# Strassen products in the first batch's second feed-forward, a third buffer of probabilities, and early loads held back

## Chip, cores and metric

One core of a Trainium2 chip runs the whole program. The metric is the device time of one execution in microseconds (us): the median of three runs is given, and one further execution was recorded by the profiler.

## What is computed

Clustered attention, then a feed-forward block, then a mixture of four experts, all in fp32, two batches of 768 tokens (8 heads of 64, model width 512). The reference, cut:

```python
mask = q_assign[:, :, :, None] == k_assign[:, :, None, :]      # argmax over 16 centroids
scores = np.where(mask, scale * q @ k.T, -1e9)
attn = softmax(scores); x = (attn @ v)                          # (1536, 512)
h = x @ w_in                                                    # 512 -> 2048
x = (h * np.clip(h + 3, 0, 6) / 6) @ w_out
p = domain_probs / domain_probs.sum(-1)
for e in range(4):
    out += p[:, e:e+1] * (np.maximum(x @ w1[e], 0) @ w2[e])     # 512 -> 1024 -> 512
```

## The kernel before

Every fp32 product of the feed-forwards is made of three f16 matmuls (high by high, high by low, low by high), so each operand is first scaled and split into a high and a low f16 half. The work stands in five stretches: attention of batch 0 (`Attn(0)`, lines 551 to 755); the first feed-forward of batch 0 (`Moe1`, line 1067, four chunks of 512 hidden columns); the second one of batch 0 (`Moe2`, line 1160, eight chunks of 512, two to an expert), with the attention of batch 1 laid between its matmuls; then `Moe1` and `Moe2` of batch 1.

In a chunk the first layer multiplies 512 inputs by 512 hidden columns for two blocks of 384 tokens. The plain way (`g1`, with `mm3`, line 949) does 2 blocks x 4 column groups x 4 input groups x 3 matmuls of 128x384, 96 in all. The class `Wino` (line 962) does the same with seven products in place of eight, 84 matmuls: `sums_w` (line 906) builds four sums of weight quarters (DVE, line 912) and splits them into `ws` (ACT, line 915; DVE, line 916), `sums_x` (line 966) builds four sums of token quarters (line 976) and splits them into `tx`, and `g1w` (line 1013) runs the products in PSUM tiles `psw`, copying partial results out (ACT into `keep`, line 1042; DVE, lines 1044 and 1049). Before the change only chunks 1 and up of the second batch use it. Both token blocks must then have one scale: `Moe1.split` (line 1148) writes the split input `x2h`, `x2l` at each block's own scale, and for batch 1 once more, as `x2hw`, `x2lw`, at the common one. The second layer (`g2`, line 1200) is 6 tiles x 12 matmuls of 128x512 into `psm`, added to `oa` by DVE (line 1218).

Attention works in sets: four matmuls (`pss`, lines 808 and 810) into a tile of two PSUM banks, a row maximum (DVE, `ut`, line 815), the exponential with its row sum (ACT, `e`, line 816), the normalised halves. In batch 0 (`turned`) the normalised row is turned by TensorE (`pst`, line 728); the normalising itself (line 716) is on POOL or DVE as the letters of `kn` say. In batch 1 (`block`) the two f16 halves `p` (lines 831 to 839) are turned by a DMA (`pt<-p`). At the start `Attn.prep` loads `raw` (q and k of a head, line 577), ACT and DVE split it into `qa`, `qb`, `ka`, `kb`, and the cluster numbers reach `qb` and `kb` through `ohq` and `pso` (lines 646 to 660). `vmax` (line 677) loads V (`vr`) and takes its largest value. `conv_w` (line 923) loads the weights of the first feed-forward (`r`, 512 KB each) and converts them.

The order on every engine is fixed when the program is built: `Order.plan` (line 244) plays the tasks through with costs of its own and places, on each engine, the task that can start first, ties and near ties by a priority; `PAR` (line 39) holds the priorities' offsets, pool sizes and choices of engine. All loads go through one queue, SP's. The engines then run these orders strictly.

Of the kernel before, what the change touches and what calls it, by code (L numbers as in the profile page):

```python
# [9 lines left out]
F32 = mybir.dt.float32  # L10
# [13 lines left out]
XSC = 8.0  # L24
# [3 lines left out]
def _f32(u):  # L28
# [14 lines left out]
    wx=4.354846549739053,  # L43
    wxs=1.369895543634687,
    wl=4.57673773750327,
    slack=0.05,
    ahead=2.5,
    wait=0,
    wait0=0.0,
    until=20.0,  # L50
    wgap=4,
    ta=33.19699973099627,
    tu=2.5993853998990764,
    lead0=23.93963461472225,
    lead2=1.4339520625967201,
    vlead2=5.517029808375997,
    lead1=2.337584274393799,
    vlead=-42.625279365213466,
    avp=-5.763899395482756,
    parts=3,  # L60
    avpa=-7.810000648567701,
    kn='PDPPDP',
    kt='AAADA',
    kb='PAAD',
    gl=["DDDD", "DDDD"],
    mx=27.33314733110412,
    sp=9.847346224163463,
    spc=7.092455914465626,
    wse=dict(i="P", o="S", **{"1": "P", "2": "A"}),
    v0=15.554800497248644,  # L70
# [9 lines left out]
    r64p=5.115084205662186,  # L80
    slow=1.0713800859542972,
    psx=3,
    dup=["SSSS", "P"],
    dpx=2,
    trp=2.509280866509063,
    trh=2,
    parta=6,
    cv0=136.14562710937315,
    cvd=15.713217770054491,
    cva=2,  # L90
    cvb=(3, 8, 4),
    wo1=0,
    two=[0, 0],
    seq=[0, 1, 3, 2, 4, 5, 6, 7, 9, 10, 11, 8],
    btail=6.718647286749997,
    bu0=40.95307569041337,
    bdu=37.26759314364028,
    bvl=14.96118549196903,
    bpr=6.461926094972937,
# [42 lines left out]
class Order:  # L142
# [101 lines left out]
    def plan(self):  # L244
# [18 lines left out]
        while left:  # L263
# [106 lines left out]
def body(ctx: ExitStack, tc: tile.TileContext, qk, vd, cent, w_in, w_out, probs, w1, w2, out):  # L370
# [36 lines left out]
    def dma(nbytes, prio, fn, r, w, lag=0.0):  # L407
        return add("SP", 0.52, prio, fn, r, w, dma=nbytes / 360e3, lag=lag)
# [32 lines left out]
    p_s = [Pool("ps_sa", 2, g_pa, True), Pool("ps_sb", 2, g_ps, True)]  # L441
# [32 lines left out]
    xv = fixed([128, B, 4], F32, "xv")  # L474
    xsc = fixed([128, B, 4], F32, "xsc")
# [51 lines left out]
    def allmax(am, n, inv, ki, unit, sc, ks, p, pp):  # L527
# [8 lines left out]
        dve(1, p, lambda: nc.vector.tensor_scalar(out=inv, in0=inv, scalar1=1e-30, scalar2=unit, op0=ALU.max, op1=ALU.mult), [], [ki])  # L536
        dve(1, p, lambda: nc.vector.reciprocal(out=sc, in_=inv), [ki], [ks])
# [13 lines left out]
    class Attn:  # L551
# [299 lines left out]
    def split_w(key, raws, p, dst=None):  # L851
        _, _, sc, ks = wcol(*key[1:])
        for k, raw in enumerate(raws):
            w = Buf(dst or (p_wi if key[1] in "i1" else p_wo), [128, 2, 512], F16, "w")
            how = PAR["wse"][key[1]]
            if how in "SPA" and (how != "S" or key[1] in "i1" and key[2] and (key[1] == "i" or key[0])):
# [4 lines left out]
                act(512, p, lambda w=w, raw=raw: nc.scalar.activation(out=w[:, 0], in_=raw.t, func=AF.Copy), [raw], [(w, 0)])  # L861
                pool(512, p, lambda w=w, raw=raw: nc.gpsimd.tensor_tensor(out=w[:, 1], in0=raw.t, in1=w[:, 0], op=ALU.subtract), [raw, (w, 0)], [(w, 1)])  # L862
# [43 lines left out]
    def sums_w(key, raws, p):  # L906
        for k in range(2):
# [5 lines left out]
            for x in (u, v):  # L913
                w = Buf(p_ws, [128, 2, 512], F16, "ws")
# [8 lines left out]
    def conv_w(key, src, p, pp):  # L923
# [3 lines left out]
        for k in range(4):  # L927
# [4 lines left out]
                out=r.t, in_=src[:, k].bitcast(I32).rearrange("p (n t) -> p n t", t=2)), [], [r])  # L932
# [29 lines left out]
    class Wino:  # L962
        bank, line = p_w, ""


        def sums_x(self, p):

            t = self.tx = [[Buf(p_tx, [128, 2, MB], F16, f"tx{i}") for _ in range(2)] for i in range(4)]
# [44 lines left out]
        def g1w(self, c, i, ts):  # L1013
# [357 lines left out]
```

## Time and profile before

| | |
|---|---|
| time, median of 3 runs | 982.29 us (979.53 to 982.61) |
| the profiled execution | 981.2 us, of which the span from the first to the last instruction is 979.3 us |
| PE matmul, PE weight load | 931.9 us (95%), 553.4 us (57%) |
| DVE, ACT, POOL | 680.0 us (69%), 622.7 us (64%), 356.8 us (36%) |
| chain that ended last | PE 67%, DVE 11%, ACT 9%, DMA 7% |
| TensorE's granted clock | 1.00 throughout |

The busy time of an engine is the union of its instructions' durations. Matmuls overlap their neighbours, so a matmul's listed duration is not what one more of them costs. DVE is VectorE, ACT ScalarE, POOL GpSimd, SP the queue that issues the DMAs.

### The profile page before, as it was taken

What the parts mean: (1) busy time and instruction counts of PE and PEld (TensorE: products, weight loads), DVE (VectorE), ACT (ScalarE), POOL (GpSimd) and SP (SyncE); (2) the same over time, 40 slices, a digit from 0 to 9 for tenths busy, and PEclk for the clock granted to TensorE, in tenths of its full rate; (3) what the DMA queues carried; (4) which work ended last, traced back from release to release, by engine and by line L of the source; (5) the groups of instructions that cost most, each with busy time, mean ns of one, the idle gap of its engine ahead of it and who ended that gap; (6) DMA issues with size and microseconds to landing.
All of it is one profiled execution on the core that took longest, in us unless ns stands there. A gap on an engine that the chain in (4) does not pass through costs nothing.

```text
span 979.3 us, 16082 instructions
## 1 busy us (share of the span) xinstructions
PE 931.9 (95%) x5699; PEld 553.4 (57%) x5699; DVE 680.0 (69%) x1427; ACT 622.7 (64%) x1243; POOL 356.8 (36%) x380
## 2 busy tenths in 40 slices
PE   2889999999999999999999999999999999999998
PEld 1667775665655655655565565556655455555554
DVE  6988896888767774674586666956589766654643
ACT  4798987768677876595496455555467455556421
POOL 0554734334534554544365221000232354344200
PEclk9999999999999999999999999999999999999999
DMA  8343438786425773484285378432111122212001
GB/s 235 88 128 85 142 104 311 265 272 229 172 98 142 152 145 124 96 168 120 61 184 127 106 140 193 141 128 69 64 65 65 56 75 87 71 59 86 1 1 65
DMA packets 123952, 120.45 MB, mean 123 GB/s; under 512 B 81440, under 2 KB 81440, under 8 KB 123872
## 3 DMA queue, kind: packets, MB, share of 16 engines
q1 hardware_dynamic: 123872, 119.43, 42.8%
q8 instruction: 45, 0.74, 0.3%
q14 instruction: 35, 0.29, 0.1%
HBM read 79.75 MB, written 14.68 MB: 96 GB/s over the span
## 4 chain that ended last, share of the span: by engine, by line
PE 67%; DVE 11%; ACT 9%; DMA 7%; issue 3%; POOL 3%; ACTq 0%; POOLq 0%; DVEq 0%; SPq 0%
PE psm L954 9%; PE psm L956 9%; PE psm L955 9%; PE psg L954 6%; PE psg L955 6%; PE psg L956 6%; PE psw L1032 4%; DMA pt<-p 4%; PE psw L1034 4%; PE psw L1033 4%; ACT e L816 3%; PE psv L744 2%; PE pst L728 2%; DVE p L839 2%; PE pss L808 2%
## 5 line engine op out<-in xcount | busy, mean ns | idle before, releaser
L862 POOL TENSOR_TENSOR w<-wraw,w 128x512 f16<-128x512 f32 x128 | 146.7, 1164 | 162.5 <-ACT w L861 128.2
L954 PE MATMUL psm<-w,h 128*128 128x512 f16 x384 | 145.8, 380 | 3.7 <-DVE oa L1218 2.5
L956 PE MATMUL psm<-w,h 128*128 128x512 f16 x384 | 145.7, 379 | 1.5 <-DVE h L1196 1.4
L955 PE MATMUL psm<-w,h 128*128 128x512 f16 x384 | 145.6, 379 | 0.0
L816 ACT ACTIVATE e<-pss,ut 128x768 f32<-128x768 f32 x96 | 86.2, 899 | 36.6 <-DVE ut L815 31.2
L954 PEld LDWEIGHTS <-w 128*128 128x128 f16 x704 | 69.4, 99 | 50.2 <-issue 7.5
L861 ACT ACTIVATE w<-wraw 128x512 f16<-128x512 f32 x128 | 77.5, 625 | 30.2 <-POOL wraw L860 16.9
L954 PE MATMUL psm<-x2h,w 128*128 128x384 f16 x288 | 94.4, 328 | 2.2 <-DVE oa L1216 1.5
L955 PEld LDWEIGHTS <-w 128*128 128x128 f16 x704 | 68.9, 98 | 48.0 <-issue 6.2
L956 PEld LDWEIGHTS <-w 128*128 128x128 f16 x704 | 68.8, 98 | 47.4 <-issue 1.8
L1218 DVE SCALAR_TENSOR_TENSOR oa<-psm,pq,oa 128x512 f32<-128x512 f32 x84 | 62.4, 746 | 47.0 <-PE psm L956 46.6
L815 DVE TENSOR_REDUCE ut<-pss 128x1 f32<-128x768 f32 x96 | 90.9, 949 | 5.8 <-PE pss L810 5.2
L955 PE MATMUL psm<-x2l,w 128*128 128x384 f16 x288 | 93.9, 326 | 0.6 <-DVE x2l L1156 0.6
L956 PE MATMUL psm<-x2h,w 128*128 128x384 f16 x288 | 93.9, 326 | 0.0
L955 PE MATMUL psg<-g,w 128*128 128x384 f16 x256 | 83.5, 326 | 0.5 <-DVE g L1106 0.5
L954 PE MATMUL psg<-g,w 128*128 128x384 f16 x256 | 83.5, 326 | 0.3 <-ACT g L1105 0.3
L860 POOL TENSOR_SCALAR wraw<-wraw,wsc 128x512 f32<-128x512 f32 x64 | 45.2, 713 | 105.3 <-DMA wraw<-in_w 37.4
L956 PE MATMUL psg<-g,w 128*128 128x384 f16 x256 | 83.5, 326 | 0.0
L808 PE MATMUL pss<-ka,qa 128*128 128x384 f32 x192 | 61.8, 404 | 8.5 <-ACT e L816 5.2
L956 PEld LDWEIGHTS <-h 128*128 128x128 f16 x384 | 37.5, 98 | 48.7 <-DVE h L1196 4.0
L954 PEld LDWEIGHTS <-h 128*128 128x128 f16 x384 | 38.2, 99 | 44.5 <-issue 3.8
L1042 ACT ACTIVATE keep<-psw 128x384 f32<-128x384 f32 x60 | 29.2, 487 | 52.9 <-PE psw L1034 52.8
(192 smaller groups left out, 2157.1 us busy)
## 6 DMA issues: line engine op xcount, KB each, us to landing
wraw<-in_w SPq DMA_DIRECT2D x128, 256.0 KB, 3.2
r<-in_w_in SPq DMA_DIRECT2D x16, 512.0 KB, 5.0
r<-in_w_out SPq DMA_DIRECT2D x16, 512.0 KB, 4.3
w<-hl_i SPq DMA_DIRECT2D x32, 256.0 KB, 3.1
w<-hl_o SPq DMA_DIRECT2D x32, 256.0 KB, 4.3
raw<-in_qk SPq DMA_DIRECT2D x16, 384.0 KB, 3.7
hl_i<-w SPq DMA_DIRECT2D x16, 256.0 KB, 3.2
hl_o<-w SPq DMA_DIRECT2D x16, 256.0 KB, 2.2
```

What stands on the lines that cost most here:

```text
L808: nc.tensor.matmul(ps[:, f, 0:HS], qa[:, qs], ka[:, f * HS:f * HS + HS], start=True, stop=False)
L815: dve(S, p, lambda: nc.vector.tensor_reduce(out=nb(), in_=ps[:, :, 0:HS], axis=AX.XY, op=ALU.max, negate=True), [ps], [(tb, n)])
L816: act(S, p, lambda: nc.scalar.activation(out=e.t.rearrange("p (a b) -> p a b", a=2), in_=ps[:, :, 0:HS], func=AF.Exp, bias=nb(), scale=1.0 ...
L860: pool(512, p, lambda raw=raw: nc.gpsimd.tensor_scalar(out=raw.t, in0=raw.t, scalar1=sc, scalar2=1.0, op0=ALU.mult, op1=ALU.mult), [ks], [ ...
L861: act(512, p, lambda w=w, raw=raw: nc.scalar.activation(out=w[:, 0], in_=raw.t, func=AF.Copy), [raw], [(w, 0)])
L862: pool(512, p, lambda w=w, raw=raw: nc.gpsimd.tensor_tensor(out=w[:, 1], in0=raw.t, in1=w[:, 0], op=ALU.subtract), [raw, (w, 0)], [(w, 1)])
L954: nc.tensor.matmul(o_, ah, bh, start=i == 0, stop=False)
L955: nc.tensor.matmul(o_, ah, bl, start=False, stop=False)
L956: nc.tensor.matmul(o_, al, bh, start=False, stop=i == 3)
L1032: nc.tensor.matmul(o_, ah, bh, start=not more and k == 0, stop=False, skip_group_check=more)
L1033: nc.tensor.matmul(o_, ah, bl, start=False, stop=False, skip_group_check=more)
L1218: dve(512, p, lambda: nc.vector.scalar_tensor_tensor(out=oa[:, t], in0=ps.t, scalar=q, in1=oa[:, t], op0=ALU.mult, op1=ALU.add), [ps, qk], ...
```

## The change

The second feed-forward of batch 0 runs chunks 2 to 7 (`w0=2`) through `g1w`. For that `Moe1.g2` makes the second block's scale the common one (`least` in `allmax`), so that only block 0 is written a second time, and pools are added: `ws0` (4), `gw0` (4) and `ps_wc`, two PSUM banks, which are taken from the attention of batch 1: its score tiles go from two to one (`psb=1`). Product 2 of a chunk goes to `psm`'s banks. Of the weights of such a chunk the half that only the sums use is not split any more (`whole`). The attention of batch 1 has three `p` buffers in place of two, and reads V a second time instead of keeping it (`vr=2`). In the plan, a DMA's buffers count as free 0.91 or 1.22 us after its end in place of 0.15, DMAs run at 340 in place of 360 bytes a ns, two of the four first V loads may not start ahead of 12.3 us and the weights' loads not ahead of 16.0 us. `kn` puts all normalising of batch 0 on POOL, `dup` two more copies of `ka`. The other numbers of `PAR` are new offsets of the plan.

```diff
-    kn='PDPPDP',
+    kn='PPPPPP',
-    b_pool=dict(raw=2, vr=4, sc=2, ..., p=2, ...),
+    b_pool=dict(raw=2, vr=2, sc=1, ..., p=3, ...),
-    dup=["SSSS", "P"],
+    dup=["PSSS", "P"],
+    vre=2, nbv=12.297, nbr=16.026, psb=1, ws0=4, gw0=4, w0=2,
...
-                b.end = max(b.end, end + 0.15)
+                b.end = max(b.end, end + (0.15 if not t.dma else 1.22 if t.cols < 0 else 0.91))
-    def dma(nbytes, prio, fn, r, w, lag=0.0):
-        return add("SP", 0.52, prio, fn, r, w, dma=nbytes / 360e3, lag=lag)
+    def dma(nbytes, prio, fn, r, w, lag=0.0, start=0.0):
+        t = add("SP", 0.52, prio, fn, r, w, dma=nbytes / 340e3, lag=lag)
+        t.ready = start
+        return t
...
-    p_s = [Pool("ps_sa", 2, g_pa, True), Pool("ps_sb", 2, g_ps, True)]
+    p_s = [Pool("ps_sa", 2, g_pa, True), Pool("ps_sb", PAR["psb"], g_ps, True)]
-    p_w = Pool("ps_w", 5, g_pf, True)
+    p_w = [Pool("ps_wc", 4 - 2 * PAR["psb"], g_ps, True), Pool("ps_w", 5, g_pf, True)]
...
+        if least:
+            dve(1, p, lambda: nc.vector.tensor_tensor(out=inv, in0=inv, in1=least[0], op=ALU.max), [least[1]], [ki])
...
+            vr = self.buf("vr", [128, 2, NT, D], F32)
+            dma(393e3, max(p(0), self.seen + 0.1 * hp), lambda: nc.sync.dma_start(out=vr.t, in_=vd[b, hp]), [], [vr])
...
+            c = 512 if whole or k > 1 else 256
...
-        split_w(key, raws, p - PAR["sp"])
+        split_w(key, raws, p - PAR["sp"], None, not sums, sums)
+        if sums:
+            sums_w(key, raws, p)
...
-                    ps = Buf(self.bank, [128, 512], F32, "psw", self.line)
+                    ps = Buf(*((p_m, [128, 512], F32, "psw", "moe") if not self.b and j == 2 else (p_w[self.b], [128, 512], F32, "psw")))
...
-                    self.split(self.x2, blk, blk, p)
-                    if b and blk == NMB - 1:
...
-                        for k in range(NMB):
-                            self.split(x2w, k, 2, p + 8 + 4 * k)
+                    self.split(x2s[b][blk], blk, blk, p)
+                    if blk:
+                        self.split(x2w[b], 0, 1, p + G["xw"][b])
...
-                load_w(key, lambda k: src[:, k], p)
+                load_w(key, lambda k: src[:, k], p, n == "1" and self.wino(c))
-        wino = lambda self, c: self.b == 1 and c > 0
-        src = lambda self: [stages[2].acc]
-        xs = lambda self: x2w
+        wino = lambda self, c: c >= (1 if self.b else PAR["w0"])
+        src = lambda self: [stages[2].acc] if self.b else self.xs()[0]
```

What this moves is seen in the orders of the engines' instructions. First ACT near the start: `qa`, `ka` split a head's q and k, `qb<-pso` puts the cluster numbers into the first pair's keys, `wconv` takes up a weight. Before:

```order
L581 ACTIVATE qa<-raw 64x768
L619 ACTIVATE sc<-psc 128x384
L592 ACTIVATE ka<-raw 64x768
L934 ACTIVATE wconv<-r_274 128x512
L581 ACTIVATE qa<-raw 64x768
L658 ACTIVATE qb<-pso 16x768 x2
L592 ACTIVATE ka<-raw 64x768
```

And now:

```order
L597 ACTIVATE qa<-raw 64x768
L635 ACTIVATE sc<-psc 128x384
L608 ACTIVATE ka<-raw 64x768
L597 ACTIVATE qa<-raw 64x768
L608 ACTIVATE ka<-raw 64x768
L674 ACTIVATE qb<-pso 16x768 x2
L597 ACTIVATE qa<-raw 64x768
```

The weight (`wconv`) has gone from ahead of the first `qb` to behind the first exponential; the third head's `qa` still stands ahead of `qb`, and its `ka` now too. On SP's queue, which issues the loads, the rows behind the first two `raw` and the probabilities were:

```order
L683 DMA vr<-in_vd 128x768 x4
L931 DMA r_274<-in_w_in 128x1024
L582 DMA qb<-qa 64x768 x2
L595 DMA ka<-ka 64x768
L577 DMA raw<-in_qk 128x768
```

and are now:

```order
L700 DMA vr<-in_vd 128x768 x2
L598 DMA qb<-qa 64x768 x2
L593 DMA raw<-in_qk 128x768 x2
L700 DMA vr<-in_vd 128x768 x2
L598 DMA qb<-qa 64x768
```

Two V loads and a weight's load of 512 KB no longer stand ahead of the third `raw`. Third, DVE in the second feed-forward of batch 0, from one row maximum (`ut<-pss`) of batch 1's attention to the next. Before:

```order
L815 TENSOR_REDUCE ut<-pss 128x1
L839 SCALAR_TENSOR_TENSOR p<-e,ut,p 128x768
L824 TENSOR_SCALAR ut<-ut 128x1
L1196 SCALAR_TENSOR_TENSOR h<-psm_5019,h 128x384
L825 RECIPROCAL ut<-ut 128x1
L815 TENSOR_REDUCE ut<-pss 128x1
```

And now, in a chunk whose weight sums fall there:

```order
L834 TENSOR_REDUCE ut<-pss 128x1
L563 RECIPROCAL wsc<-wv 128x1
L934 TENSOR_TENSOR wraw<-wraw 128x256
L858 SCALAR_TENSOR_TENSOR p<-e,ut,p 128x768
L843 TENSOR_SCALAR ut<-ut 128x1
L934 TENSOR_TENSOR wraw<-wraw 128x256
L844 RECIPROCAL ut<-ut 128x1
L934 TENSOR_TENSOR wraw<-wraw 128x256 x2
L834 TENSOR_REDUCE ut<-pss 128x1
```

Four sums of weight quarters now lie between two maxima that had one `h` between them.

## Rows read from the trace of the kernel before

**Rows 1.** The page, busy time: engine, us (share of the span), instructions.
```profile
PE 931.9 (95%) x5699; PEld 553.4 (57%) x5699; DVE 680.0 (69%) x1427; ACT 622.7 (64%) x1243; POOL 356.8 (36%) x380
```
**Rows 2.** Stretches: length, busy us (x instructions) of PE, PEld, DVE, ACT, POOL; clock; DMA.
```profile
25.00:137.00 112.00, 103.37 (x729) 78.77 (x721) 99.44 (x235) 98.76 (x216) 61.10 (x63) 1.00 0.37 109
137.00:278.00 141.00, 137.34 (x870) 84.49 (x869) 110.40 (x229) 106.48 (x225) 55.44 (x68) 1.00 0.65 224
278.00:612.00 334.00, 325.31 (x2077) 191.51 (x2075) 221.66 (x453) 220.16 (x434) 142.63 (x146) 1.00 0.58 136
```
**Rows 3.** Timeline of PE, 479.7 to 484.9 us: start, duration, instruction.
```profile
479.85 0.33 PE L955 MATMUL psm<-x2l,w 128*128 128x384 f16 x1
...
481.31 0.33 PE L955 MATMUL psm<-x2l,w 128*128 128x384 f16 x1
```
**Rows 4.** Timeline of PE, ACT and DVE at the start: start, duration, instruction [idle before].
```profile
14.53 0.82 PE L653 MATMUL pso<-ident_b,ohq 128*128 128x128 bf16 x6 [5.48 <-DVE ohq L646]
...
21.87 1.01 PE L810 MATMUL pss<-kb,qb 80*128 80x384 f32 x2 [2.58 <-DVE kb L660]
...
8.83 0.33 SPq L577 DMA_DIRECT2D raw<-in_qk  x1
...
19.16 0.84 ACT L581 ACTIVATE qa<-raw 64x768 fp32r<-64x768 f32 x1 [3.13 <-DMA raw<-in_qk]
20.03 0.80 ACT L658 ACTIVATE qb<-pso 16x768 fp32r<-16x768 bf16 x1
```
**Rows 5.** The page, DMA issues: KB each, median us from issue to landing.
```profile
raw<-in_qk SPq DMA_DIRECT2D x16, 384.0 KB, 3.7
```
**Rows 6.** Groups of instructions: busy us, mean ns | idle before. Normalising in batch 0's attention.
```profile
L716 POOL TENSOR_SCALAR e<-e,ut 128x768 f32<-128x768 f32 x36 | 35.2, 984 | 42.9 <-ACT pt L735 12.8 <-DVE ut L824 10.4 <-DVE ut L825 8.0
L716 DVE TENSOR_SCALAR e<-e,ut 128x768 f32<-128x768 f32 x12 | 7.8, 649 | 0.1
```
**Rows 7.** Groups, whole run: the kinds of work that the change adds or cuts.
```profile
L862 POOL TENSOR_TENSOR w<-wraw,w 128x512 f16<-128x512 f32 x128 | 146.7, 1164 | 162.5 <-ACT w L861 128.2
L956 PE MATMUL psm<-x2h,w 128*128 128x384 f16 x288 | 93.9, 326 | 0.0
L912 DVE TENSOR_TENSOR wraw<-wraw 128x256 f32<-128x256 f32 x80 | 31.6, 424 | 1.4 <-POOL w L862 1.0
L1042 ACT ACTIVATE keep<-psw 128x384 f32<-128x384 f32 x60 | 29.2, 487 | 52.9 <-PE psw L1034 52.8
L916 DVE TENSOR_TENSOR ws<-wraw,ws 128x512 f16<-128x512 f32 x40 | 26.7, 691 | 0.2 <-ACT ws L915 0.2
L915 ACT ACTIVATE ws<-wraw 128x512 f16<-128x512 f32 x40 | 23.1, 621 | 21.8 <-DVE wraw L912 20.3 <-DVE p L839 1.3
L1049 DVE TENSOR_TENSOR psw<-psw,keep 128x384 f32<-128x384 f32 x40 | 22.4, 561 | 18.0 <-PE psw L1034 17.6 <-ACT keep L1042 0.3
L1156 DVE SCALAR_TENSOR_TENSOR x2l<-acc,xsc,x2h 128x384 f16<-128x384 f32 x16 | 8.8, 610 | 0.2 <-ACT x2h L1154 0.2
```
**Rows 8.** Line L976: ns min/median/max, first and last start.
```profile
L976 DVE TENSOR_TENSOR keep<-x1h,keep x4: 541/543/865, 619.5 to 633.9; 128x384 f32<-128x384 f16 x4
```
**Rows 9.** Timelines of PE, DVE and ACT, 487.6 to 490.8 us: one score set.
```profile
487.60 0.65 PE L808 MATMUL pss<-ka,qa 128*128 128x384 f32 x2
...
488.64 0.96 DVE L815 TENSOR_REDUCE ut<-pss 128x1 f32<-128x768 f32 x1
...
489.70 0.90 ACT L816 ACTIVATE e<-pss,ut 128x768 f32<-128x768 f32 x1 [0.82 <-DVE ut L825]
...
490.28 0.65 PE L808 MATMUL pss<-ka,qa 128*128 128x384 f32 x2
```
**Rows 10.** Waits of PE, 278 to 612 us: us in total, times, longest us.
```profile
PE psv L790 <- DMA pt<-p: 2.6, 3, 1.2
PE psm L954 <- DVE oa L1218: 2.5, 3, 1.2
```
**Rows 11.** Wait of ACT, 278 to 612 us.
```profile
ACT p L835 <- DMA pt<-p: 11.6, 10, 2.6
```

More of the change, by code (lines that the diff above doesn't have):

```diff
@@ L42 @@
     wsl="DD",
-    wx=4.354846549739053,
-    wxs=1.369895543634687,
-    wl=4.57673773750327,
+    wx=-1.1522284557866715,
+    wxs=1.4523186816394191,
+    wx0=43.37150067903462,
+    wl=7.46084025153843,
     slack=0.05,
+    vre=2,
+    nbv=12.297071615165793,
+    nbr=16.02553508875921,
+    xw=[4.0, 8.0],
     ahead=2.5,
     wait=0,
-    wait0=0.0,
+    wait0=0.8,
     until=20.0,
     wgap=4,
[L52 to L59, printed above, removed]
+    ta=33.594464710837215,
+    tu=2.610847985583524,
+    lead0=24.37119650954177,
+    lead2=1.612592269486031,
+    vlead2=-5.510083383690325,
+    lead1=2.0943943567986207,
+    vlead=-47.653832407507394,
+    avp=-10.148156292544726,
     parts=3,
-    avpa=-7.810000648567701,
-    kn='PDPPDP',
+    avpa=-4.563255851914643,
+    kn='PPPPPP',
     kt='AAADA',
-    kb='PAAD',
+    kb='AAPD',
     gl=["DDDD", "DDDD"],
-    mx=27.33314733110412,
-    sp=9.847346224163463,
-    spc=7.092455914465626,
+    mx=28.217289639625243,
+    sp=15.01076876764054,
+    spc=8.604011088911196,
     wse=dict(i="P", o="S", **{"1": "P", "2": "A"}),
-    v0=15.554800497248644,
+    v0=9.16094046643471,
     lr=0.3,
@@ L92 @@
     wo1=0,
-    two=[0, 0],
[L94 to L99, printed above, removed]
+    psb=1,
+    ws0=4,
+    gw0=4,
+    w0=2,
+    wr=8,
+    wob=8,
+    two=[0, 0],
+    seq=[0, 1, 3, 2, 5, 4, 6, 7, 9, 10, 11, 8],
+    btail=7.85293067823645,
+    bu0=40.446540415353034,
+    bdu=31.34254887856145,
+    bvl=4.7901688951714965,
+    bpr=6.264441884379736,
 )
@@ L682, in vmax @@
                 self.pair[hp]["vr"] = vr
-                dma(393e3, p(hp), lambda hp=hp, vr=vr: nc.sync.dma_start(out=vr.t, in_=vd[b, hp]), [], [vr])
+                dma(393e3, p(hp), lambda hp=hp, vr=vr: nc.sync.dma_start(out=vr.t, in_=vd[b, hp]), [], [vr], start=0.0 if b or hp < G["vre"] else G["nbv"])
                 dve(S, p(hp), lambda hp=hp, vr=vr: nc.vector.tensor_reduce(
@@ L888, in raw_w, with load_w @@
         return raws
-    def load_w(key, src, p):
+    def load_w(key, src, p, sums=False):
         raws = raw_w(src, p - 4 - PAR["mx"])
@@ L931, in conv_w @@
             dma(524e3, p - PAR["r64p"], lambda r=r, k=k: nc.sync.dma_start(
-                out=r.t, in_=src[:, k].bitcast(I32).rearrange("p (n t) -> p n t", t=2)), [], [r])
+                out=r.t, in_=src[:, k].bitcast(I32).rearrange("p (n t) -> p n t", t=2)), [], [r], start=G["nbr"])
             a = lambda raw=raw: raw.t.bitcast(I32)
@@ L943, in conv_w @@
             act(512, p, lambda k=k, raw=raw: nc.scalar.activation(
-                out=mxj.t, in_=raw.t, func=AF.Square, accum_out=am[:, k:k + 1]), [raw], [(am, k)], acc=True)
+                out=mxj, in_=raw.t, func=AF.Square, accum_out=am[:, k:k + 1]), [raw], [(am, k)], acc=True)
         norm(am, wcol(*key[1:]), p, pp)
-        split_w(key, raws, p - PAR["spc"], p_stg)
+        split_w(key, raws, p - PAR["spc"], p_stg, keep=key[1] == "i" and key[2] > 0)
     def mm3(p, out, n, lhs, rhs, reads, after=()):
@@ L962, in body @@
     class Wino:
-        bank, line = p_w, ""
         def sums_x(self, p):
-            t = self.tx = [[Buf(p_tx, [128, 2, MB], F16, f"tx{i}") for _ in range(2)] for i in range(4)]
+            b = self.b
+            self.tx = [Buf(p_tx if b else p_x2["hl"[i % 2]], [128, 2, 2, MB], F16, f"tx{i}") for i in range(4)]
             src, at = self.src(), [p]
@@ L1176, in load, with xs @@
                 raws = raw_w(lambda k: src[:, k], p - 4)
-                split_w(key, raws, p)
+                split_w(key, raws, p, None, n == "2" or not self.wino(c), n == "1" and self.wino(c))
                 if n == "1" and self.wino(c):
                     sums_w(key, raws, p)
-        wino = lambda self, c: self.b == 1 and c > 0
-        src = lambda self: [stages[2].acc]
-        xs = lambda self: x2w
+        wino = lambda self, c: c >= (1 if self.b else PAR["w0"])
+        src = lambda self: [stages[2].acc] if self.b else self.xs()[0]
+        def xs(self):
+            q = [x2w[self.b], x2s[self.b][1]]
+            return [lambda r, j, n=n: q[j][n][:, r] for n in range(2)], [x for y in q for x in y]
         def g1(self, c, blk, f, p):
@@ L1267, in body @@
         if st.wino(c):
-            if c == 1:
-                todo[st].append((st.sums_x, (start[st] + G["wx"] + (14.0 if two else 0.0),)))
+            if not st.wino(c - 1):
+                todo[st].append((st.sums_x, ((start[st] + G["wx"] + (14.0 if two else 0.0)) if st.b else t - G["wx0"],)))
             todo[st].append((st.load, (c, st.names[0], t - G["wl"])))
-            G3 = 1.04
+            G3 = 1.04 * slow
             cut = len(tail) // 2 if prev[0].wino(prev[1]) else len(tail) - 1
```

116 lines of the change are left out of this document (58 added, 58 removed).

## The prediction

> **What bounds the kernel now.** I read the page's busy times first, then the busy time by stretch, then single matmuls on the timeline, then the waits. By the page PE is busy for 95% of the span [rows 1], and the stretches say where. From 137 us to 278 us (first feed-forward of batch 0) and from 278 us to 612 us (second feed-forward, with batch 1's attention) PE is busy 137.34 of 141 us and 325.31 of 334 us; DVE, ACT and POOL have room there, DVE 221.66 of 334 [rows 2]. From 25 to 137 us (batch 0's attention) it is otherwise: DVE 99.44 and ACT 98.76 of 112 us are in use together and PE has 8.6 us free [rows 2]; there a row's way through DVE, ACT and DVE again sets the pace. Ahead of that lies a start in which everybody waits for loads. So three questions decide: what a matmul less gives, whether the start gets shorter, and whether the stretch from 278 us stays PE's when DVE gets the sums.
>
> **Fewer matmuls.** Six chunks go from 96 to 84 matmuls of 128x384 in the first layer: 72 fewer. A listed matmul of this form lasts 326 ns [rows 7], but that is its way through the array; what one costs is the step to the next. Nine steps of a full run take 481.31 - 479.85 = 1.46 us, 162 ns each [rows 3]. So 72 x 0.162 = **11.7 us** of PE's time go. All lie in the stretch that is PE's now, so they shorten it as long as the rest keeps up.
>
> **The start.** The third `raw` (head 3's q and k) is issued at 8.83 us and lets ACT go on at 19.16 us, 10.3 us later [rows 4], where the median load of this kind lands in 3.7 us [rows 5]: four V loads and a weight of 512 KB were queued ahead. On ACT that `qa` stands in front of `qb<-pso`, whose input `pso` was done at 14.53 + 0.82 = 15.35 us, but which ran at 20.03 us; the first score's second half follows at 21.87 us [rows 4]. Now two V loads and that weight stand behind this load. With a landing as the median has it, `raw` is there near 13 us, and `qb` waits for `pso` alone: at most 20.03 - 15.35 = 4.7 us earlier. At least nothing comes of it, if the next stretch, where DVE and ACT are full, takes up the work that was done in the gaps (V's maxima, the weights' conversion). I take **-4.0 us**, near the upper end, since most of what is put off is a load and two or three operations of a microsecond.
>
> **Normalising.** Twelve operations of 649 ns leave DVE, 7.8 us in all, and join POOL at 984 ns each [rows 6], 11.8 us; POOL has 112 - 61.1 us free in that stretch [rows 2]. ACT, as full as DVE, is not relieved, so between 0 and -7.8 us I take **-1.0 us**, near ACT's end. The two copies of `ka` that go to POOL leave two short DMAs out and I count them at nothing; POOL's free time covers them.
>
> **What the second feed-forward gets in return.** DVE: eight quarter sums in each of six chunks, 48 x 0.424 = 20.4 us; 24 low halves of `ws` x 0.691 = 16.6; in `g1w` 36 additions from PSUM x 0.561 = 20.2; four operations x 0.610 = 2.4 for the block written a second time [rows 7]; 28 operations of `sums_x` x 0.543 = 15.2 [rows 8]. That is 75 us on top of 221.66 [rows 2]: 296 us in 334 - 11.7 = 322 us, **92%**. ACT gets 36 copies x 0.487 = 17.5 and 24 high halves x 0.621 = 14.9 us [rows 7], some 6 us for 12 operations on `tx` and `x2hw`, and loses part of 26 halved splits: about 250 of 322 us. POOL loses 26 half splits, some 26 x 0.58 = 15 us (half of 1164 ns) [rows 7]. No wait of the old stretch is near such a load: PE's idle time there is 334 - 325.3 = 8.7 us [rows 2], the largest entries 2.6 us for turned probabilities and 2.5 us for `oa` [rows 10]. The third `p` buffer takes away what ACT waits for that DMA, 11.6 us [rows 11], but ACT's wait was covered by PE's other matmuls, and I count it at nothing beyond PE's own 2.6 us.
>
> With one score tile in place of two, a set can't start before the exponential of the one before has read it. One set: matmuls from 487.60, maximum from 488.64 to 489.60, exponential from 489.70 to 490.60, so 3.0 us; before, the next set began at 490.28, after 2.7 us [rows 9]. The new order puts more feed-forward matmuls between two sets, mostly 12 to 18. Twelve of 384 columns are 1.9 us beside a set's own 0.8, and then PE waits; eighteen of them, or twelve of 512 columns, cover it. What stands behind a waiting set on PE are the feed-forward's matmuls. The nearest rows bound the new waits from none (or -2.6 us, if the old DMA wait goes and nothing comes) to the share that PE idles where DVE is 89% in use: 8.6 of 112 us, of 322 us 24.8, which is 16 us more than now [rows 2]. I take **+4 us**, nearer the old stretch's rows, since most of the added DVE work has slack of a whole chunk (some 30 us of matmuls) before PE needs it.
>
> The rest I count at nothing. Four operations less on ACT and DVE where batch 1's second feed-forward begins: they lay beside matmuls. Four more V loads: the queue moved data for 58% of that stretch [rows 2]; a landing without cover would be some 4 us each [rows 5], ahead of batch 1's probabilities only.
>
> **The sum**: -11.7 - 4.0 - 1.0 + 4.0 = **-12.7 us**. Against the profiled execution's 981.2 us this is 968.5. The median of the runs stands 1.1 us above that execution, so I expect a median of **969.6 us**.
>
> **Rivals.** *DVE becomes the bound.* If PE idles in the new stretch as it does between 25 and 137 us, the +4 becomes +16: 968.5 + 12 + 1.1 = **981.6 us**, no change. For it: 92% is above that stretch's 89%, and POOL gets in DVE's way: an operation with two inputs in SBUF takes 543 ns, once 865 [rows 8]. Against: in that stretch ACT was as full as DVE, here it has a fifth free. If each of the 104 added operations of this sort met POOL like the slowest, they would cost 104 x 0.32 = 33 us more, 329 us in 322. That is what the Trainium skill would make of it in the worst case ("SBUF — State Buffer", Who interferes with whom): DVE instructions with two SBUF inputs contend with GpSimd instructions that read SBUF, and the loser blocks for the whole instruction. The trace agrees as to the sort of operation; its median of 543 ns says that few meet.
>
> *One score tile stalls every set.* DVE's order now has four quarter sums and a `p` between two maxima, 4 x 0.42 us and a split, so a maximum can come late, and with one tile each lateness stops PE. At half a microsecond for each of batch 1's 48 sets it is 24 us in place of 4: 968.5 + 20 + 1.1 = **989.6 us**, slower. It decides from (11.7 + 4 + 1) / 48 = 0.35 us a set. For it: some sets are 12 narrow matmuls apart, 2.8 us against 3.0. Against: with the sets 3 to 4 us apart DVE's queue between them is no longer than the gap. The Trainium skill has this as a sign ("Perfetto Trace Analysis", Optimization Strategy): the same gap over and over on the engine that should be full can mean too few buffers in PSUM. No row before shows such a gap, because there were two tiles.
>
> *Everything comes.* The start gives 4.7, DVE's relief 7.8, and no wait is added: -24.2 us, **958.1 us**. For it: DVE idles little between 25 and 137 us. Against: ACT does no less there.
>
> **How the numbers follow.** My forecast has a chance of 0.6, with 963 to 977 us as its own range (new waits from none to 11 us); DVE as the bound 0.2, the stalled sets 0.1, everything 0.1. A measurement of this kernel tells some 0.3%, 2.9 us, from no change: faster is below 979.3, slower above 985.2. Faster: 0.6 + 0.1 + 0.06 of the DVE case = 0.76; same 0.13; slower 0.1 + 0.01 = 0.11. The range of **960 to 983 us** takes in the forecast and the DVE case and leaves out the stalled sets and half of the best case.
>
> **What would show it.** Right: `qb<-pso` near 15.5 us; the first `psg` some 4 to 5 us earlier than at 137 us; from the first `psm` to the last attention row of batch 1 some 7 to 8 us less than 334 us, with DVE near 90%. Wrong: PE's waits for `pss` on `e` grow past 5 us (one tile), waits on `oa`, `h`, `tx` or `ws` past 10 us (DVE), or the first feed-forward begins no earlier, the start's gain spent in batch 0's attention.

## The result, and the profile after

| | median | lowest to highest |
|---|---|---|
| before, 5 runs | 981.16 us | 979.53 to 982.61 |
| after, 5 runs | 971.42 us | 969.13 to 975.48 |

The ratio is 0.9904, with an interval of 0.9875 to 0.9934: faster by 1%. The profiled execution took 969.13 us (span 967.4), 12.1 us less than the one of before; it is the fastest of its five, that of before the middle one, and between the medians lie 9.7 us. The page of after has these busy times, to be read against [rows 1]:

```profile
PE 923.6 (95%) x5627; PEld 545.8 (56%) x5627; DVE 737.5 (76%) x1551; ACT 646.5 (67%) x1311; POOL 361.6 (37%) x394
```

72 matmuls are gone, and TensorE is busy 8.3 us less, not 11.7. DVE has 57.5 us more. The stretches of after that answer to [rows 2] (length, then busy time of PE, PEld, DVE, ACT, POOL; granted clock; DMA share and GB/s):

```profile
25.00:129.00 104.00, 99.26 (x709) 75.86 (x707) 90.54 (x215) 96.85 (x215) 65.91 (x71) 1.00 0.39 117
129.00:271.60 142.60, 137.74 (x874) 85.04 (x873) 110.34 (x228) 106.47 (x223) 56.39 (x70) 1.00 0.63 217
271.60:600.00 328.40, 316.98 (x2000) 183.31 (x1999) 288.27 (x595) 248.13 (x506) 139.40 (x146) 0.99 0.61 144
```

In the first, PE idles 4.7 us where it idled 8.6. In the third it idles 11.4 us, more than the 8.7 of before, and its clock was not full throughout. Taking the starts of four matmuls from the timelines, the two executions divide like this:

```
                                                before   after   difference
start to the first psg (first ff of batch 0)     137.1   129.1      -8.1
first psg to first psm (second ff of batch 0)    140.7   142.5      +1.8
first psm to last psg (end of batch 1's first)   459.1   454.5      -4.5
last psg to last psm                             238.2   236.9      -1.3
```

One score set (four matmuls, 0.8 us) that stood ahead of the first `psg` stands behind it now: so much of the first two differences is work that changed sides.

**The start.** The timeline of after, for [rows 4]:

```profile
7.64 3.07 SPq L593 DMA_DIRECT2D raw<-in_qk  x2
...
11.87 0.84 ACT L597 ACTIVATE qa<-raw 64x768 fp32r<-64x768 f32 x1 [3.21 <-DMA raw<-in_qk]
...
13.53 0.82 PE L669 MATMUL pso<-ident_b,ohq 128*128 128x128 bf16 x6 [4.78 <-DVE ohq L662]
...
15.37 1.63 ACT L674 ACTIVATE qb<-pso 16x768 fp32r<-16x768 bf16 x2 [1.79 <-DVE kb L676]
```

`raw` lets `qa` go on at 11.87 us instead of 19.16, and `qb` runs at 15.37 instead of 20.03. The times of before are those of one execution, though. one_tile_before, an experiment below, has before's order on every engine up to 315 us, and in its execution the third `raw` landed 2 us earlier; its `qb` and its first exponential:

```profile
17.97 0.80 ACT L658 ACTIVATE qb<-pso 16x768 fp32r<-16x768 bf16 x1
...
23.78 0.90 ACT L816 ACTIVATE e<-pss,ut 128x768 f32<-128x768 f32 x1
```

So the new order brings `qb` 2.6 to 4.7 us forward, and the first exponential (21.91 us in after, 25.84 in before) 1.9 to 3.9.

**The second feed-forward of batch 0.** PE's waits there, for [rows 10]:

```profile
PE psn L559 <- ACT scrap L914: 4.4, 3, 2.3
PE psm L976 <- DVE h L1217: 2.5, 1, 2.5
PE pss L827 <- ACT e L835: 1.6, 2, 0.9
```

No wait comes back at every set. Two are long, that of `psm` and the longest of three of `psn`. The first stands at 284 us. On the timeline:

```profile
281.25 2.13 ACT L1171 ACTIVATE x2h<-acc,xsc 128x384 f16<-128x384 f32 x4 [0.93 <-DVE xsc L553]
...
283.29 2.12 ACT L1171 ACTIVATE x2hw<-acc,xsc 128x384 f16<-128x384 f32 x4
...
284.02 2.20 DVE L1173 SCALAR_TENSOR_TENSOR x2lw<-acc,xsc,x2hw 128x384 f16<-128x384 f32 x4
285.31 0.47 ACT L1216 ACTIVATE h<-psm 128x384 f16<-128x384 f32 x1
286.14 0.55 DVE L1217 SCALAR_TENSOR_TENSOR h<-psm,h 128x384 f16<-128x384 f32 x1
286.74 0.38 PE L976 MATMUL psm<-w,h 128*128 128x512 f16 x1 [2.52 <-DVE h L1217]
```

The input of the second feed-forward written a second time (`x2hw`, `x2lw`, new with this change) stands ahead of the fourth `h` on ACT and on DVE. PE's order has nothing ahead of the matmul that needs this `h`, and it waits 2.52 us. The second is at 363 us:

```profile
356.50 1.44 SPq L796 DMA_TRANSPOSE pt<-p  x1
358.03 1.80 SPq L905 DMA_DIRECT2D wraw<-in_w  x3
...
365.13 0.63 ACT L914 ACTIVATE scrap<-wraw 128x512 bf16<-128x512 f32 x1 [1.08 <-DMA wraw<-in_w]
...
365.91 0.39 PE L559 MATMUL psn<-am,ones 128*128 128x4 f32 x2 [2.28 <-ACT scrap L914]
```

Three of four loads of a weight (`wraw`) wait on SP's queue for a transpose of probabilities. The squares of the weight (`scrap`) come late, and so does the small sum `psn` that PE does from them. Behind both waits the clock fell; short windows, columns as above:

```profile
284.00:287.00 3.00, 0.47 (x5) 0.28 (x4) 2.91 (x8) 3.00 (x6) 0.62 (x1) 1.00 0.99 369
287.00:288.50 1.50, 1.50 (x10) 0.44 (x12) 1.40 (x2) 1.45 (x3) 0.54 (x1) 0.76 0.52 176
288.50:290.00 1.50, 1.50 (x9) 0.24 (x10) 1.47 (x2) 1.11 (x2) 0.00 (x0) 0.50 0.88 262
290.00:291.50 1.50, 1.50 (x5) 0.54 (x4) 1.44 (x3) 1.43 (x4) 0.03 (x1) 0.60 0.90 184
...
366.00:367.50 1.50, 1.50 (x6) 0.77 (x7) 0.88 (x3) 1.50 (x5) 0.65 (x2) 0.60 1.05 395
367.50:369.00 1.50, 0.92 (x4) 0.35 (x3) 0.63 (x2) 0.70 (x3) 1.24 (x2) 0.50 1.01 379
369.00:370.50 1.50, 1.50 (x8) 0.81 (x8) 1.50 (x4) 1.44 (x5) 0.00 (x0) 0.77 1.29 215
```

0.50 is 1.2 GHz in place of 2.4. The three windows from 287 us lose 1.5 x (0.24 + 0.50 + 0.40) = 1.7 us, those from 366 us as much.

### The profile page after: what moved, and what is told of

Its sections match the earlier page's. It is cut to its first block, busy times and chain, and to the rows that moved or that the text cites. A ratio compares the mean times of both kernels' runs of the same rounds, so it can differ in the third digit from the quotient of the medians.

```text
span 967.4 us, 16161 instructions
## 1 busy us (share of the span) xinstructions
PE 923.6 (95%) x5627; PEld 545.8 (56%) x5627; DVE 737.5 (76%) x1551; ACT 646.5 (67%) x1311; POOL 361.6 (37%) x394
## 4 chain that ended last, share of the span: by engine, by line
PE 46%; DVE 6%; ACT 3%; DMA 1%; issue 1%; POOL 1%; SPq 0%; POOLq 0%; ACTq 0%
PE psm L976 6%; PE psm L977 6%; PE psm L978 6%; PE psw L1053 6%; PE psw L1055 6%; PE psw L1054 6%; PE psg L977 2%; PE psg L978 2%; PE psg L976 2%; PE pss L827 1%; DMA wraw<-in_w 1%; PE psv L809 1%; PE pss L829 1%; DVE h L1217 1%; ACT e L835 1%
## 5 line engine op out<-in xcount | busy, mean ns | idle before, releaser
L882 POOL TENSOR_TENSOR w<-wraw,w 128x512 f16<-128x512 f32 (+1 forms) x128 | 136.1, 1083 | 188.9 <-ACT w L881 146.9
L976 PE MATMUL psm<-w,h 128*128 128x512 f16 x384 | 146.1, 381 | 2.7 <-DVE h L1217 2.5
L978 PE MATMUL psm<-w,h 128*128 128x512 f16 x384 | 146.1, 380 | 0.5 <-DVE h L1217 0.5
L834 DVE TENSOR_REDUCE ut<-pss 128x1 f32<-128x768 f32 x96 | 91.3, 952 | 11.2 <-PE pss L829 9.8
L1063 ACT ACTIVATE keep<-psw 128x384 f32<-128x384 f32 x96 | 46.6, 486 | 60.1 <-PE psw L1055 59.5
L881 ACT ACTIVATE w<-wraw 128x512 f16<-128x512 f32 (+1 forms) x128 | 71.7, 580 | 21.2 <-POOL wraw L880 12.4
L880 POOL TENSOR_SCALAR wraw<-wraw,wsc 128x512 f32<-128x512 f32 x64 | 48.3, 762 | 98.3 <-DVE ws L938 30.8
L976 PE MATMUL psg<-g,w 128*128 128x384 f16 x256 | 83.5, 326 | 1.4 <-DVE t L1124 1.2
L977 PEld LDWEIGHTS <-w 128*128 128x128 f16 x512 | 50.1, 98 | 36.6 <-issue 5.4
L978 PEld LDWEIGHTS <-w 128*128 128x128 f16 x512 | 50.1, 98 | 36.0 <-issue 3.0
L976 PEld LDWEIGHTS <-w 128*128 128x128 f16 x512 | 50.7, 99 | 33.4 <-issue 1.7
L1217 DVE SCALAR_TENSOR_TENSOR h<-psw,h 128x384 f16<-128x384 f32 x78 | 42.9, 552 | 27.8 <-ACT h L1216 27.6
L978 PEld LDWEIGHTS <-h 128*128 128x128 f16 x384 | 37.6, 98 | 46.3 <-DVE h L1217 1.0
L1054 PE MATMUL psw<-tx,ws 128*128 128x384 f16 x192 | 63.0, 328 | 0.8 <-DVE tx L1005 0.8
L1053 PE MATMUL psw<-tx,ws 128*128 128x384 f16 x192 | 63.1, 328 | 0.7 <-ACT tx L1004 0.6
L1055 PE MATMUL psw<-tx,ws 128*128 128x384 f16 x192 | 63.0, 328 | 0.0
```

The lines of the kernel that those rows point to most:

```text
L834: dve(S, p, lambda: nc.vector.tensor_reduce(out=nb(), in_=ps[:, :, 0:HS], axis=AX.XY, op=ALU.max, negate=True), [ps], [(tb, n)])
L881: act(c, p, lambda w=w, raw=raw, c=c: nc.scalar.activation(out=w[:, 0, 0:c], in_=raw[:, 0:c], func=AF.Copy), [raw], [(w, 0)])
L882: pool(c, p, lambda w=w, raw=raw, c=c: nc.gpsimd.tensor_tensor(out=w[:, 1, 0:c], in0=raw[:, 0:c], in1=w[:, 0, 0:c], op=ALU.subtract), [raw ...
L976: nc.tensor.matmul(o_, ah, bh, start=i == 0, stop=False)
L977: nc.tensor.matmul(o_, ah, bl, start=False, stop=False)
L978: nc.tensor.matmul(o_, al, bh, start=False, stop=i == 3)
```

## The experiments

Each median is compared with runs of the kernel before on the same chip. Where an edit changes a number or a pool, the plan is made anew and all orders with it; where tasks are moved in the finished plan, all else keeps its place. `delay(t, us)` puts a task, and what depends on it, behind the tasks up to `us` later in the plan.

**again**: the change as it is.

> The changed kernel once more, its instructions in the same order, as the measure for the others on this chip. Both theories: 971 us, within 2 us; granted clock 0.996, with PE at half clock for some 3.5 us after each of its two longest waits (2.5 us near 284 us, 2.3 us near 364 us).

Measured: 970.38 us, 0.9898 (0.9879 to 0.9917). This profile had 2.8 us more in the first feed-forward (145.3) and 2.3 less from there to the last `psg` (452.2): single stages move by two to three us between executions, and their sum by less. The clock is part of it: in this execution 1.7 us are lost at half clock in the first feed-forward, from 220.7 us on, and behind 284 us only once.

**feed_first, sums_later, both_moved**: the two waits of batch 0's second feed-forward, by moving what is late or what waits.

```diff
     o.plan()
+    for x in reversed(again):       # the tasks that write x2hw, x2lw of batch 0
+        delay(x, 6.0)
+    for x in sums[8:]:              # PE's psn tasks
+        delay(x, 3.0)
```

The first loop alone is feed_first, the second sums_later (less than 3.0 where buffers forbid it), both both_moved.

> Only the eight ACT and DVE operations that write block 0 a second time (x2hw, x2lw) are moved behind the next h; all else keeps its order. Theory (single misplaced waits, each made dearer by the clock): PE's wait near 284 us falls from 2.5 to about 0.6 us, and the half clock after it goes, so 1.9 + 1.7 = 3.6 us less than the repeated changed kernel. Rival (the stretch is DVE's now, 88% busy): the wait turns up again within the next 50 us, less than 1 us is won.

> Only the small matmuls that sum a weight's squares (psn), with what hangs on them, are moved by up to 3 us behind matmuls that are ready; all else keeps its order. Theory: PE's three waits for squares of late weights (2.3, 1.0 and 1.1 us) go, and with the first the half clock from 366 to 369.5 us: 4.4 + 1.7 = 6 us less. Rival (DVE): under 1.5 us, other waits grow as much.

> Both moves together. Theory: they add up, 9 to 10 us less than the repeated changed kernel, near 962 us, granted clock 1.000. Rival (DVE): less than 3 us.

Measured: 969.8 us, 0.9884 (0.9869 to 0.9899); 979.92 us, 0.9983 (0.9969 to 0.9997); 979.94 us, 1.0004 (0.9989 to 1.0019). The first did not try its theory. `h` went ahead on ACT, but on DVE the four `x2lw` still stood in front, as its timeline shows:

```profile
285.26 0.47 ACT L1218 ACTIVATE h<-psm 128x384 f16<-128x384 f32 x1
...
286.27 2.21 DVE L1173 SCALAR_TENSOR_TENSOR x2lw<-acc,xsc,x2hw 128x384 f16<-128x384 f32 x4 [0.20 <-ACT x2hw L1171]
288.40 0.55 DVE L1219 SCALAR_TENSOR_TENSOR h<-psm,h 128x384 f16<-128x384 f32 x1
289.00 0.38 PE L976 MATMUL psm<-w,h 128*128 128x512 f16 x1 [2.81 <-DVE h L1219]
```

sums_later gave up the whole gain. PE's waits from 270 to 600 us in it:

```profile
PE pss L827 <- ACT e L835: 5.3, 6, 2.0
PE psw L1053 <- ACT keep L1063: 4.9, 4, 2.3
```

No `psn` is waited for any more. But the weight is still late: ACT, which must square it, holds up `keep`, and PE waits 2.3 us for that in place of `psn`. There what is late is the load, and PE's place in the queue only decides which wait shows it. That led to h_and_loads_first, below. A second cost is new. What hangs on the moved sums is late too: ACT, whose order is unchanged, waits 20.8 us in 18 pieces for POOL's scaled weights (273 to 610 us; again 12.1 in 11), and PE's longest wait for `e` stands behind two of these. From the first `psm` to the last `psg` the run takes 464.3 us where again takes 452.2: PE idles 7.0 us more, and 5.1 us more are lost at half clock.

**loads_early** and **dve_normalises**: the holding back of loads undone (all four V loads and the weights' may start at once), and the normalising.

```diff
-    vre=2, nbr=16.026,
+    vre=4, nbr=0.0,
```
```diff
-    kn='PPPPPP',
+    kn='PDPPDP',
```

> The changed kernel with the early loads not held back: all four V loads and the weights' loads may start at once; the plan is made anew with that. Theory (the start gave some 4 us, since loads stood ahead of the third raw): third raw lands 5 us or more later than in the changed kernel, first psg at 133 us or later in place of 129.1 us, the whole 3 to 5 us longer. Rival (the relief of DVE gave all 8 us by which the first psg came earlier): first psg within 1.5 us of 129.1.

> The changed kernel with 12 of batch 0's 48 normalisations back on DVE (7.8 us of DVE's time between 25 and 129 us), planned anew. Theory as predicted (ACT is as full, so the relief is worth some 1 us): first psg at 130 to 131 us, the whole 1 to 2 us longer. Rival (DVE alone sets the pace there): first psg at 133 us or later, the whole 4 us longer or more.

Measured: 980.36 us, 0.9996 (0.998 to 1.0011), the first `psg` at 141.1 us, 12.0 later than in after; and 978.99 us, 0.9986 (0.9972 to 1.0), the first `psg` at 132.6, 3.5 later, and the first feed-forward 150.3 us long instead of 142.5. Of dve_normalises' 3.5 us, 1.7 are lost at half clock from 78.7 us on; its first feed-forward has a wait of 2.7 us for DVE and half clock once, which after has not. In loads_early `qb` ran at 15.28 us, as early as in after: what is lost comes behind it. The stretch up to the first `psg`, then the timeline at PE's longest wait in it:

```profile
25.00:141.00 116.00, 103.06 (x719) 78.01 (x719) 96.49 (x221) 98.74 (x216) 66.60 (x71) 0.99 0.37 110
```
```profile
44.44 0.63 ACT L965 ACTIVATE scrap<-wconv 128x512 bf16<-128x512 f32 x1 [1.57 <-DVE wconv L963]
...
45.06 0.47 ACT L754 ACTIVATE pt<-pst 128x384 f32<-128x384 f32 x1
...
45.59 0.55 PE L747 MATMUL pst<-ident,e 128*128 128x128 f32 x3 [2.95 <-ACT pt L754]
```

PE idles 12.9 us there, 4.7 in after; for `pt` alone it waits 5.4 us, 0.5 in after. ACT stands in front of a weight's squares that DVE has not prepared, the probabilities' copy `pt` stands behind them, and PE waits 2.95 us for that, with half clock behind it. From 25 to 45 us DVE has 9.4 us of the weights' operations, 5.4 in after. Weights that come early are converted early, on the two engines that set the pace.

**one_tile_before**: the kernel before, with one score tile for batch 1.

```diff
-    p_s = [Pool("ps_sa", 2, g_pa, True), Pool("ps_sb", 2, g_ps, True)]
+    p_s = [Pool("ps_sa", 2, g_pa, True), Pool("ps_sb", 1, g_ps, True)]
```

> The kernel before with one score tile in place of two for batch 1's attention, nothing else, planned anew: what the single tile costs by itself. Theory (feed-forward matmuls fill the time, a few tenths of a us a set at most): 981 to 985 us. Rival (half a us for each of 48 sets): 24 us, near 1005 us.

Measured: 978.21 us, 0.9974 (0.9958 to 0.999), no slower. PE's wait for `e` between 278 and 612 us grew from 0.5 to 3.9 us in six pieces, `psv` and `psm`, with 5.9 us less, gave back more. The first `psg` came 1.9 us earlier, but not by the new plan, whose order differs only from 315 us on: so much the landings of the first loads move from one execution to another.

**plain_batch0**: the change without Strassen products in batch 0 (72 matmuls more).

```diff
-    w0=2,
+    w0=8,
```

> The changed kernel without Strassen products in batch 0 (all eight chunks plain), one score tile and the other parts kept, planned anew. Theory (72 matmuls are 11.7 us, of which new waits and half clock give 5 back): first psg unchanged near 129 us, first psm to batch 1's last attention row 333 us or more against 327 us, the whole near 978 us, 6 to 8 us longer. Rival (the matmuls' gain is lost to DVE and the whole gain came before 272 us): within 2 us of the changed kernel's 971 us.

Measured: 971.66 us, 0.9903 (0.9873 to 0.9932), the same as after within some 3 us; from the first `psm` to the last `psg` 453.7 us, 454.5 in after. All that is gained without those products comes from the other parts: the first `psg` at 129.0 us as in after, and less waiting behind it (PE waits 0.8 us for turned probabilities from the first `psm` to the last `psg`, and not for `oa`). The plan's new figures for DMAs are in this kernel as in all others made from the change, and so are the new offsets; neither was tried by itself. They are the main rival to what is put down to single parts below.

**two_p_buffers**: `p=3` back to `p=2` in the change.

> The change with two buffers of probabilities again (order planned anew). By the prediction's step (third buffer worth nothing beyond PE's own 2.6 us): 970 to 974 us, ACT waiting for pt<-p some 10 us again. Rival (with DVE and ACT fuller the third buffer carries the gain): 975 to 982 us, PE waiting for psv or pss 5 us or more longer.

Measured: 974.29 us, 0.9927 (0.991 to 0.9944), 0.3 us above the range of the prediction's step and below the rival's. ACT waits for `pt<-p` 19.2 us from the first `psm` to the last `psg`, 8.4 of them at line 854 (longest 3.7), where after has 7.2. What PE waits for most from the first `psm` to the last `psg` is new:

```profile
PE psw L1053 <- ACT keep L1063: 3.9, 5, 1.8
PE pss L827 <- ACT e L835: 3.3, 8, 0.9
```

That ACT is late with `keep`, which the Strassen products need, because it stood for a `p` buffer is not shown: its waits for `pt<-p` end at 327, 335, 419 and 574 us and later, PE's longer ones for `keep` at 368, 370, 446 and 545. At 446 us, the longest, ACT squares a weight ahead of `keep`. The third buffer is worth 3 to 4 us here (974.29 less 971.42 and 970.38), new plan included.

**h_first, h_and_loads_first**: the two waits again, at their roots.

```diff
     o.plan()
+    for x in loads:                 # wraw's loads: on SP ahead of transposes placed before
+        ahead(x)                    # them, as far up as their buffer was free in the plan
+    for t in fourth_h:              # its ACT and its DVE task
+        front(t)                    # ahead of x2hw, x2lw
```

h_first has the second loop alone.

> The change, with the last high and low half of the first chunk's fourth h tile put ahead of x2hw, x2lw on ACT and DVE (two operations moved, the plan's order kept otherwise). Theory: the Strassen term of 11.7 us is eaten by a few single waits and the half clock behind them; the wait for h (2.5 us at 284 us) and the half clock after it (some 1.5 to 2 us) then go, so 966 to 969 us, no gap over 1 us and no clock below 0.9 between 284 and 292 us. Rival (the wait only moves: sums_x, the next chunk's keep or ws come later by as much): 970 to 972 us, the 2.5 us found again behind psw, keep or psm.

> As h_first, and on SP's queue the loads of raw weights (wraw) of batch 0's second feed-forward put ahead of those transposes of probabilities that had been placed before them though the buffers were free. Theory: the waits of psn for the squares (4.4 us in 3) and the half clock behind the first go too: 962 to 966 us. Rival (the queue's order is not what makes the loads late, or the later transposes stall psv by as much): within 1.5 us of h_first, with psv waiting for pt<-p 2 us or more.

Measured: 970.47 us, 0.9888 (0.987 to 0.9906); and **967.63 us**, 0.9856 (0.9836 to 0.9875), the fastest of all. In h_first the 2.5 us at 284 us were gone and no clock fell there, but the time did not follow: waits of 0.4, 1.1 and 1.6 us stand behind it, up to 303 us, where after had 0.6 in one, and `psn` still waited 2.4 us, with the half clock after it. With the loads moved as well, SP's queue reads:

```profile
352.18 2.30 SPq L905 DMA_DIRECT2D wraw<-in_w  x4
357.88 1.75 SPq L796 DMA_TRANSPOSE pt<-p  x1
```

The four loads start at 352 us, not three of them at 358. The two places in windows:

```profile
284.00:292.00 8.00, 7.80 (x39) 3.11 (x38) 7.66 (x13) 7.88 (x15) 1.63 (x1) 1.00 0.75 251
363.50:371.00 7.50, 6.42 (x43) 3.35 (x42) 7.38 (x16) 6.71 (x21) 3.53 (x4) 1.00 0.86 217
```

The clock is full in both. Of `psn`'s 4.4 us, 0.9 are left.

**plain_h_first**: plain_batch0 with the same `front` as h_first (`w0=8`).

> As plain_batch0 (no Strassen in batch 0), with the fourth h tile put ahead of x2hw, x2lw as in h_first; plain_batch0 had no wait of psn, so no load is moved. It is the match to h_and_loads_first: both without their waits of over 2 us. Theory (the twelve matmuls a chunk less are eaten not by those few waits alone but by many small ones, and by second-layer matmuls that come slower): 969 to 971.5 us, so Strassen in batch 0 is worth 1.5 to 4 us. Rival (the single waits were all that ate it): it stays at 971.5 to 974 us or above, 4 us and more behind h_and_loads_first. Second rival (Strassen in batch 0 is worth nothing): 967 to 968.5 us.

Measured: 970.28 us, 0.9886 (0.9867 to 0.9904). Against its match of 967.63 the Strassen products of batch 0 are worth 2.7 us of the 11.7 (the two intervals overlap a little), less if one adds that this kernel still writes `x2hw` and `x2lw`, which nothing reads in it. From the first `psm` to the last `psg`, plain_h_first:

```profile
272.90:726.90 454.00, 447.94 (x2831) 264.54 (x2829) 314.96 (x638) 293.71 (x570) 164.60 (x167) 1.00 0.54 129
```

and h_and_loads_first:

```profile
272.90:725.10 452.20, 440.48 (x2757) 256.88 (x2756) 377.19 (x774) 318.80 (x637) 160.93 (x167) 1.00 0.53 129
```

7.5 us less of PE's busy time make the stretch 1.8 us shorter. The waits of PE over it, largest first, plain_h_first:

```profile
PE psm L976 <- DVE h L1219: 1.2, 2, 1.0
PE psam L545 <- DVE h L1219: 1.1, 1, 1.1
PE psm L976 <- DVE oa L1239: 1.1, 1, 1.1
```

and h_and_loads_first:

```profile
PE pss L827 <- ACT e L835: 1.9, 3, 0.9
PE psam L545 <- DVE h L1219: 1.6, 1, 1.6
PE psv L809 <- DMA pt<-p: 1.1, 1, 1.1
PE psm L976 <- DVE oa L1239: 1.1, 1, 1.1
PE psw L1053 <- ACT keep L1063: 0.9, 1, 0.9
PE psn L559 <- ACT scrap L914: 0.9, 1, 0.9
```

The whole lists add up to 5.9 us in 9 waits and to 11.2 us in 17. So with both large waits gone, 5.3 us of the 11.7 still go into small waits of one or two microseconds. Another 4.6 us (11.7 - 1.8 - 5.3) the list of waits does not show. The matmuls' starts place nearly all of them, taken as steps from start to start without the listed waits: those of 128x384 in f16 take 10.1 us less, not 11.7; the 576 of the second layer 1.9 us more (216.9 ns a step, 213.6 without the products); scores, values and small sums 1.2 us more. Whether these are waits too short for the list, since a matmul is listed at twice its step, stays open, and the two kernels have different plans.

## Why the prediction was right, and where its steps were off

The total came near the forecast, 971.42 us where it had 969.6: -9.7 us between the medians and -12.1 between the profiled executions, where the sum had -12.7. The terms did not come as forecast, and that their errors cancel is luck. By stages: up to the first `psg` -8.1 us, where start and normalising had -5.0; in the first feed-forward +1.8, where it had nothing; from the first `psm` to the last `psg` -4.5, where it had -7.7, and -5.4 in plain_batch0, which has no product there; behind that -1.3 for nothing. The sign named for the second feed-forward came near, 326.9 us from the first `psm` to the last attention row, 6.5 less than before; but plain_batch0, with 331.7 us there, needs 122.0 from that row to the last `psg` where after needs 127.6: the products bring the row forward and leave more work behind it.

- **Fewer matmuls, -11.7: the count was right, the effect was mis-sized.** The same kernel without them runs in the same time (971.66 and 971.42 us), and with the large waits removed they are worth 2.7 us. The step that failed is "they shorten it as long as the rest keeps up": the rest kept up on average and not in single places.
- **New waits, +4: too small, and of another kind.** I asked whether DVE would be full, and it is 288 of 328 us, 88% where I had 92%; `pss` waits for `e` 1.6 us, under the 5 that I had named. What cost was the order behind two events that the prediction counted only as load: four low halves "x 0.610 = 2.4 for the block written a second time" cost PE 2.5 us because they stand ahead of `h`, and loads of weights that it does not speak of came late behind a transpose. The two are 4.8 us of waiting and 3.4 us lost at half clock; with both taken away the kernel gains 2.8 to 3.8 us (970.38 and 971.42 to 967.63). From the first `psm` to the last `psg` PE idles 13.1 us, 10.1 in before and 7.1 in plain_batch0; with the clock's 3.4 us the term is 6.4 against before and 9.4 against the match without the products.
- **The start, -4.0: right in kind, its size in part luck.** `qb` ran at 15.37 us (forecast 15.5), 4.7 earlier, and the first exponential at 21.91 in place of 25.84, 3.9 earlier. But both are reckoned from the one execution that the forecast was read from; against one_tile_before, the same order once more, they are 2.6 and 1.9. And that is what the new order gives; loads_early has the same `qb` without the holding back. What holding back gives is the quiet behind the start, which I had put down only as a risk to this term: with the loads early the stretch takes 12 us more, new plan included.
- **Normalising, -1.0: too small, if the plan is not the cause.** Undone it costs 3.5 us up to the first `psg`, new plan and 1.7 us of half clock included; 3.9 from the start and 3.5 from here would make 7.4 of the 8.1 us. Then that ACT "is not relieved" was the wrong bound, and of 7.8 us less of DVE at most nearly half pass on. Which of the two it is stays open.
- **Counted at nothing.** The third `p` buffer is worth 3 to 4 us, new plan included; by which wait is not shown. The first feed-forward took 1.8 us more, and the last stretch 1.3 us less. The 1.8 are the least of it: ten kept executions have after's order up to there and took 142.5 to 146.1 us, before and one_tile_before 140.7 both. Three of the ten (again, plain_batch0, two_p_buffers) lost 1.7 us there at half clock.
- **What undoing a part can't tell.** loads_early, dve_normalises and two_p_buffers lose 8.9, 7.6 and 2.9 us against after, 19.4 together, twice the whole gain of 9.7. Each has a new plan with offsets that were not set anew for it, so these losses are not shares of the gain.
- **Rivals.** *DVE becomes the bound*: no; nor did POOL get in its way more than before. The Trainium skill's rule ("SBUF — State Buffer", Who interferes with whom) would have shown in the operations with two SBUF inputs; by the trace their medians are unchanged, 416 ns (417 before) for the 128x256 sums, 683 (681) for the low halves of `ws`, with a longest of 1661 (1072). *One tile stalls every set*: no, 1.6 us in two waits, and the kernel before with one tile is no slower. *Everything comes*: the start did, the matmuls did not.

## What to carry to other kernels

Before a count of saved instructions goes into a sum, undo just that count in the finished kernel: here the part with the clearest arithmetic was worth a quarter of it at best, and the kernel without it is as fast. Which of the other parts, with the plan made for them, carried the gain can't be had by undoing them one at a time. On a bound engine at 95% look for single waits of two microseconds, not for the mean load of the others (one taken away gave nothing by itself here, both gave some 3 us); ask for each new group of operations what now stands behind it on its queue. And where a late input shows as a wait, move the input, not the instruction that waits: moving the latter cost 9 us, moving the loads gained 3.

## What was not expected of the hardware

The granted clock fell to half behind waits of PE of 2.28 and 2.52 us, and the way back took some 4 us, so that the wait of 2.52 us cost some 4.2: full before 284 us, 0.76, 0.50, 0.60 in the three windows from 287 to 291.5 us. It fell behind shorter waits too. two_p_buffers had ten slow matmuls behind a wait of 1.83 us at 219.26, and plain_batch0 had them behind two of about one microsecond:

```profile
218.77 0.32 PE L976 MATMUL psg<-g,w 128*128 128x384 f16 x1 [0.94 <-DVE t L1124]
...
221.07 0.38 PE L976 MATMUL psg<-g,w 128*128 128x384 f16 x1 [1.17 <-ACT wconv L956]
```
```profile
221.20:224.70 3.50, 3.50 (x12) 1.61 (x11) 1.42 (x3) 2.60 (x7) 1.35 (x3) 0.51 0.45 182
```

And it did not follow every long one: plain_batch0 had 2.53 us at 287.69 with no slow matmul behind it, feed_first 2.81 us at 286.19. The Trainium skill ("TensorE: Matmul & The Clock Gate", HAM oscillation) says that idle gaps can send TensorE back to the slow clock and that the work after them starts slow; the trace agrees as to the kind, with gaps of these lengths. The executions of after had mean clocks of 0.990 to 0.996 and took 969.13 to 975.48 us, the slowest at the lowest clock; of h_and_loads_first's four, three had 1.0. What decides whether a wait costs the clock stays open.
